# Quarter loads, an earlier first transpose and other k^T v portions in an attention and expert kernel

## The chip, the cores and the metric

The kernel runs on one core of one Trainium2 chip. The metric is the device time of one execution in microseconds (us). Engines: TensorE (PE; its weight loads are listed as PEld), VectorE (DVE), ScalarE (ACT), GpSimd (POOL), and SyncE (SP), which here does nothing but issue DMAs.

## What is computed

Linear attention with an RMS norm, then a mixture of experts with one expert for each token and a skip test. In short:

```python
kv  = einsum('bhsd,bhse->bhde', k, v)        # q, k, v: (8, 8, 576, 64) float32
o   = einsum('bhsd,bhde->bhse', q, kv)
x   = o / sqrt(mean(o*o, -1) + 1e-6) * g_norm   # then as (4608, 512)
run = x @ w_skip > 0
e   = argmax(x @ w_gate); gate = softmax(x @ w_gate)[e]
out = x + run * gate * (relu(x @ w1[e]) @ w2[e])   # 8 experts, 512 -> 1024 -> 512
```

## The kernel before

The program has two parts. The attention part takes the first 124 us of the span; the expert part takes the rest and is not touched. The order of all instructions is written out by hand (`tc.manual_schedule`): each engine works through its own queue in the order in which the program issues.

**Loads.** For each of the eight b (batches), k, v and q come as tiles `[128, 4, 9, 64]`: index j = 2u + w counts pairs of heads, and a row of one j is 9 x 64 numbers in one stretch (2,304 bytes). `load_part` (L115) moves half of such a tile, u = 0 or 1, in one DMA of 576 KB. `load_kv` (L128) issues k and v by turns, `load_q` (L136) q. All loads and most stores are on SyncE's queue. k and v have three buffers each, q has two. b = 0, 1, 2 of k and v and b = 0, 1 of q are issued at the start; the rest from the plan below.

**k^T v.** `state(b, some)` (L371) works through 18 pairs (u, c) for a b, four products for each into `sum_ps`; the first nine need u = 0 of k and v, the others u = 1. The last portion ends with ScalarE's copies into a `kvd` buffer (L386). Three short steps finish the buffer: `state_t(b)` (L389) transposes (L393) and copies (L396), `state_m(b)` (L399) multiplies by the gate weights (L402) and copies (L405), `state_s(b)` (L407) puts the result into the other half of the partitions (L411, L415).

**The 36 units.** A unit n is a fourth of a b's rows and heads; units 16, 17, 34 and 35 take the ninth column c of four b at once, from `q8s`, and need no transpose of their own. b = 0 to 7 begin at units 0, 4, 8, 12, 18, 22, 26 and 30. `turn(n)` (L451) transposes q on TensorE into the one bank of `ps_q` (L460) and copies on ScalarE (L463). `values(n)` (L486) multiplies it with `kvd` (L498, or L508 for the ninth column) into one of two banks, ScalarE squares (L514), `squares` sums on VectorE (L522), `root` is on ScalarE (L529), `norm` takes the reciprocal (L536) and the product `xl` (L545) on VectorE, which frees the bank. GpSimd adds up the logits and weighs `xl` (L597 to L615). Rows of `xb` are stored.

**The plan.** The loop over steps n (L1007) issues `turn(n + 1)`, `root(n - 1)`, the jobs "early", `values(n)`, `norm(n - 1)`, `squares(n)`, the jobs "pe", then the gating pieces for VectorE (from step 12 on for the first group, from step 22 for the second) and the jobs "end". `portions` (L963) says at which step the k^T v of a b begins and how many of its 18 pairs each step takes, at "pe". In the step after the last portion come `state_t` (early) and `state_m` (pe), a step later `state_s`. `load_kv(b + 3)` is at the "end" of the step with `state_t(b)`, `load_q(b + 2)` two steps after the b's first unit.

Ahead of the loop stand, on TensorE, filler products (`dense`), the two halves of `state(0)`, and then `turn(0)`, `state_t(0)`, `state_m(0)`, `turn(1)`, `state_s(0)` (L953 to L961).

Of the kernel before, what the change touches and what calls it, by code (L numbers as in the profile page):

```python
# [8 lines left out]
FP32 = mybir.dt.float32  # L9
# [8 lines left out]
def kernel(  # L18
# [44 lines left out]
    B, H, S, D = q.shape  # L63
    DM = H * D
    N = B * S
    P = 128
    C = S // 64
# [30 lines left out]
    kv_pool = attn.enter_context(tc.tile_pool(name="kv", bufs=3))  # L98
# [13 lines left out]

    kts, vts, qts = {}, {}, {}

    def load_part(t, src, b, u):  # L115

        js = slice(2 * u, 2 * u + 2)
        nc.sync.dma_start(
            out=t[:, js, :, :].rearrange("p j c d -> p j (c d)"),
            in_=src[b].rearrange("(j a) (p c) d -> (a p) j (c d)", a=2, c=C)[:, js, :])  # L120

    def load(pool, tag, src, b):
        t = pool.tile([P, 4, C, D], FP32, tag=tag, name=tag)
        for u in range(2):
            load_part(t, src, b, u)
        return t

    def load_kv(b):  # L128
        if b < B:
            for name, to in (("k", kts), ("v", vts)):  # L130
                to[b] = kv_pool.tile([P, 4, C, D], FP32, tag=name, name=name)
            for u in range(2):
                for src, t in ((k, kts[b]), (v, vts[b])):
                    load_part(t, src, b, u)

    def load_q(b):  # L136
        if b < B:
            qts[b] = load(q_pool, "q", q, b)
# [4 lines left out]


    load_kv(0)
    load_q(0)

# [19 lines left out]
    def dense(count, ps=warm_ps):  # L167

        for _ in range(count):
            nc.tensor.matmul(out=ps[:, :], lhsT=ones[:, :],  # L170
                             rhs=ones[:, :].unsqueeze(1).to_broadcast([P, 4, P]), start=True, stop=True)
# [33 lines left out]
    for i in range(KVD):  # L205
        t = kvd_pool.tile([P, 2, 2, 2, PK], FP32, name=f"kvd{i}")
# [87 lines left out]
    for lo, m, _ in runs:  # L294

        if m < P and (lo, m) not in again:
            t = keep.tile([P, P], FP32, name=f"again{lo}_{m}")
# [73 lines left out]
    def state(b, some):  # L371

        kt, vt = kts[b], vts[b]
        for i in some:
            u, c = divmod(i, C)
            for w in range(2):
                for a in range(2):
                    r = slice(a * 64, (a + 1) * 64)
                    nc.tensor.matmul(  # L379
                        out=sum_ps[w * 64:(w + 1) * 64, a, u, :],  # L380
                        lhsT=kt[r, 2 * u + w, c, :], rhs=vt[r, 2 * u + w, c, :],
                        start=(c == 0), stop=(c == C - 1), skip_group_check=True)
        if some.stop < 2 * C:
            return
        for w in range(2):
            nc.scalar.copy(out=own(b, w)[:, :, G:G + 2 * D].rearrange("p u (a d) -> p a u d", a=2),  # L386
                           in_=sum_ps[w * 64:(w + 1) * 64, :, :, :])

    def state_t(b):  # L389
        for u in range(2):  # L390
            for w in range(2):
                r = slice(w * 64, (w + 1) * 64)
                nc.tensor.matmul(out=kvT_ps[:, u, r], lhsT=kvds[b % KVD][:, u, w, w, G:G + 2 * D],  # L393
                                 rhs=ident[:, r], start=True, stop=True)
        kvT = att_pool.tile([P, 2, P], FP32, tag="kvT", name="kvT", bufs=1)
        nc.scalar.copy(out=kvT[:, :, :], in_=kvT_ps)  # L396
        kvTs[b] = kvT

    def state_m(b):  # L399
        kvT = kvTs.pop(b)  # L400
        for u in range(2):
            nc.tensor.matmul(out=lg_ps[:, u, :, :, :], lhsT=kvT[:, u, :], rhs=gw_b[:, u, :, :, :],  # L402
                             start=True, stop=True)
        for w in range(2):
            nc.scalar.copy(out=ends_of(own(b, w)), in_=lg_ps[w * 64:(w + 1) * 64, :, :, w, :])  # L405

    def state_s(b):  # L407

        for w in range(2):
            r, o = slice(w * 64, (w + 1) * 64), slice((1 - w) * 64, (2 - w) * 64)  # L410
            nc.tensor.matmul(out=sw_ps[o, :], lhsT=ident[r, r], rhs=own(b, w), start=True, stop=True,  # L411
                             skip_group_check=True)
        for w in range(2):
            o = slice((1 - w) * 64, (2 - w) * 64)
            nc.scalar.copy(out=kvds[b % KVD][o, :, w, 1 - w, :],  # L415
                           in_=sw_ps[o, :].rearrange("p (u k) -> p u k", u=2))
# [25 lines left out]
    def at(step, part, job):  # L442
        todo.setdefault((step, part), []).append(job)
# [7 lines left out]
    def turn(n):  # L451
        _, b, i, u = units[n]
        if i is None:
            qTs[n] = q8s[b][:, u, :, :, :]
            return
        ps = ps_q.tile([P, 2, 2, 2, 64], FP32, tag="q", name="q_ps")
        for w in range(2):
            for hf in range(2):
                c = 4 * i + 2 * hf
                nc.tensor.transpose(out=ps[:, w, :, hf, :], in_=qts[b][:, 2 * u + w, c:c + 2, :],  # L460
                                    identity=ident[:, :])
        qT = att_pool.tile([P, 2, 2, P], FP32, tag="qT", name="qT")
        nc.scalar.copy(out=qT[:, :, :, :].rearrange("p w a t -> p (w a t)"),  # L463
                       in_=ps[:, :, :, :, :].rearrange("p w a h t -> p (w a h t)"))
        qTs[n] = qT
# [353 lines left out]
    def slot_rows(cols, pool, tag):  # L819

        n = cols.stop - cols.start
        rows = pool.tile([P, n], I32, tag=f"rows{tag}", name="rows")
        nc.vector.tensor_single_scalar(out=rows[:, :], in_=srow[:, cols], scalar=float(N),
                                       op=ALU.add)
        src = pool.tile([P, n], I32, tag=f"src{tag}", name="src")
        nc.vector.scalar_tensor_tensor(out=src[:, :], in0=rows[:, :], scalar=N, in1=rows[:, :],
                                       op0=ALU.is_lt, op1=ALU.mult)
        return rows, src
# [64 lines left out]
    def early():  # L893
# [41 lines left out]
        yield "mid", put  # L935

    load_kv(1)
    load_q(1)
    load_kv(2)


# [8 lines left out]
    for n, (_, b, i, _) in enumerate(units):  # L950
        if i is not None:
# [2 lines left out]
    dense(4)  # L954
    state(0, range(C, 2 * C))
    dense(5)
    turn(0)
    state_t(0)
    state_m(0)
    turn(1)  # L960
    state_s(0)  # L961

    portions = {1: (1, (10, 8)), 2: (4, (6, 6, 6)), 3: (7, (5, 6, 7)), 4: (11, (3, 4, 4, 4, 3)),  # L963
                5: (16, (3, 2, 6, 7)), 6: (20, (4, 4, 5, 5)), 7: (24, (4, 4, 5, 5))}
    over = 0
    for b, n in starts.items():
        if b:
            step, counts = portions[b]
            i = 0
            for count in counts:  # L970
                at(step, "pe", lambda b=b, some=range(i, i + count): state(b, some))
                i += count
                step += 1
            assert i == 2 * C and step < n and step - len(counts) > over - 1
            at(step, "early", lambda b=b: state_t(b))
            at(step, "pe", lambda b=b: state_m(b))
            at(step + 1, "early" if step + 1 == n else "pe", lambda b=b: state_s(b))
            over = step
        at(over, "end", lambda b=b: load_kv(b + 3))

        at(n + 2, "end", lambda b=b: load_q(b + 2))

    def gating(g):

        yield from choose(g)
        yield lambda: rank(g)
        numbers = number(g)
        yield next(numbers)
        if g == LAST - 1:
            yield from rank_experts()  # L990
            load_weights(0, wpool_a, later=True)
        yield from numbers
        if g == LAST - 1:
            yield from early()
# [57 lines left out]
    with tc.tile_pool(name="wpool_b", bufs=1, reuse_waits="tile") as wpool_b, \  # L1052
# [491 lines left out]
        rows, src = slot_rows(slice(0, NCOL), gat_pool, "")  # L1544
# [34 lines left out]
        with tc.If(n_rounds > 1):  # L1579
            with tc.For_i(1, n_rounds, 1):  # L1580
# [12 lines left out]
                rows, src = slot_rows(slice(0, NCOL), slot_pool, "")  # L1593
# [35 lines left out]
```

## Time and profile before

| | |
|---|---|
| three runs | 375.22, 376.25, 376.61 us (median 376.25) |
| the profiled execution | 376.26 us |
| its span, first to last instruction | 374.4 us |
| TensorE clock granted | 0.996 |
| busy: PE, PEld, DVE, ACT, POOL | 97%, 84%, 65%, 39%, 33% |
| k, v, q loads: number, size | 16 each, 576 KB |
| median from issue to landing: k, v, q | 9.9, 10.7, 10.2 us |

A profile page has the busy share of each engine, the span in 40 slices of 9.4 us, a chain of work followed back from the last instruction, and groups of instructions by line. In a line of the timeline the first number is the start, the second the length from the first instruction to the end of the last, then engine, line, operation and tiles, how many, and in brackets how long the engine was idle ahead of it and what ended that.

### The profile page before, as it was taken

The page shows a single profiled execution, that of the slowest core. Times are in us where ns is not written, and L with a number is a line of the kernel's source. Part 1 is how long each engine was busy: PE and PEld are TensorE (multiplying, and loading weights), DVE is VectorE, ACT ScalarE, POOL GpSimd, SP SyncE. Part 2 cuts the span into 40 slices and gives each one's busy share as a digit, 9 for nine tenths or more (in the row PEclk, how much of TensorE's full clock was granted, in tenths as well). Part 3 has the DMA queues.
Part 4 walks back from the last instruction along what each step waited for, and adds up shares of the span by engine and source line. Part 5 has one row for each costly group of instructions (what it writes and reads, how often), then busy time and mean ns, then how long its engine had stood idle before and what let it go on. Part 6 is the DMA issues. An engine that isn't in the chain of part 4 may idle for free.

```text
span 374.4 us, 9661 instructions
## 1 busy us (share of the span) xinstructions
PE 363.2 (97%) x3859; PEld 315.2 (84%) x3859; DVE 244.3 (65%) x627; ACT 146.0 (39%) x398; POOL 123.1 (33%) x191
## 2 busy tenths in 40 slices
PE   8999999999999999999999999999999999999994
PEld 4687797898979679779879987988998998998983
DVE  2354458667878845676766675876876876878831
ACT  2366676676776222214403421430440440441420
POOL 7035457655768555223012303203202302102003
PEclk9999999999999999999999999999999999999998
DMA  7999999996499449966518263672762761700001
GB/s 290 393 391 391 401 403 394 404 384 201 130 330 311 111 109 325 395 204 226 203 53 268 69 226 103 225 254 54 259 228 47 273 230 61 269 3 32 26 1 53
DMA packets 32039, 81.70 MB, mean 218 GB/s; under 512 B 2474, under 2 KB 2482, under 8 KB 31988
## 3 DMA queue, kind: packets, MB, share of 16 engines
q1 hardware_dynamic: 28176, 69.47, 52.3%
q0 software_dynamic: 3792, 11.53, 9.2%
q8 instruction: 32, 0.52, 0.6%
q14 instruction: 19, 0.16, 0.1%
q10 hardware_dynamic: 20, 0.02, 0.0%
HBM read 66.80 MB, written 14.48 MB: 217 GB/s over the span
## 4 chain that ended last, share of the span: by engine, by line
PE 83%; issue 6%; POOL 4%; DVE 3%; ACT 3%; POOLq 0%; DVEq 0%; ACTq 0%
PE bank L1253 44%; PE bank L1185 9%; PE o_ps L498 7%; PE sum_ps L379 5%; PE bank L1173 4%; PE q_ps L460 3%; PE g_ps L393 2%; PE q_ps L170 2%; PE bank L1154 2%; POOL xb L615 2%; DVE xl L545 1%; DVE rs L522 1%; PE g_ps L411 1%; ACT qT L463 1%; ACT sq L514 1%
## 5 line engine op out<-in xcount | busy, mean ns | idle before, releaser
L1263 ACT COPY p<-bank 128x128 f32<-128x128 f32 (+6 forms) x70 | 20.8, 297 | 99.5 <-PE bank L1253 88.2
L1253 PE MATMUL bank<-xt,w 128*128 128x128 f32 (+5 forms) x336 | 55.5, 288 | 0.0
L615 POOL TENSOR_TENSOR xb<-xl,g_b 128x512 f32<-128x512 f32 x36 | 43.7, 1216 | 34.3 <-DVE rs L536 30.4
L1384 POOL DMA_INDIRECT out_dram<-xg,rows x14 | 14.0, 999 | 118.6 <-DVE xg L1381 115.4
L1253 PEld LDWEIGHTS bank<-xt,w 128*128 128x128 f32 x336 | 47.0, 190 | 1.9 <-DVE bank L1257 1.4
L1257 DVE TENSOR_TENSOR bank<-bank,p 128x128 f32<-128x128 f32 (+6 forms) x70 | 23.6, 338 | 30.2 <-PE bank L1253 29.0
L498 PE MATMUL o_ps<-kvd,qT 128*128 128x146 f32 x240 | 35.8, 290 | 1.0 <-ACT kvd L415 0.7
L1253 PE MATMUL bank<-xs,s 128*128 128x128 f32 (+5 forms) x224 | 36.7, 289 | 0.0
L522 DVE TENSOR_REDUCE rs<-sq 128x8 f32<-128x512 f32 x36 | 24.6, 682 | 15.6 <-ACT sq L514 15.5
L498 PEld LDWEIGHTS o_ps<-kvd,qT 128*128 128x128 f32 x240 | 31.6, 188 | 2.0 <-ACT kvd L415 1.5
L1253 PEld LDWEIGHTS bank<-xs,s 128*128 128x128 f32 x224 | 31.1, 190 | 1.0 <-ACT p L1263 0.8
L1185 PE MATMUL bank<-w,ht 128*32 128x128 f32 (+2 forms) x424 | 29.9, 313 | 0.0
L545 DVE TENSOR_TENSOR xl<-o_ps,rs 128x584 f32<-128x584 f32 x32 | 24.5, 767 | 4.3 <-DVE rs L536 0.5
L1185 PEld LDWEIGHTS bank<-w,ht 128*32 128x32 f32 (+2 forms) x424 | 18.2, 119 | 10.7 <-issue 7.6
L1253 PE MATMUL bank<-t,ht 128*128 128x256 f32 x112 | 27.0, 384 | 0.0
L1145 POOL DMA_INDIRECT xg<-out_dram,src x14 | 15.6, 1116 | 33.3 <-DMA out_dram<-xg,rows 18.0
L1253 PE MATMUL bank<-w,ht 128*128 128x256 f32 x112 | 26.5, 380 | 0.0
L514 ACT ACTIVATE sq<-o_ps 128x512 f32<-128x512 f32 x34 | 20.3, 597 | 15.0 <-PE o_ps L498 14.4
L379 PE MATMUL sum_ps<-v,k 64*64 64x64 f32 x1152 | 25.3, 227 | 0.4 <-issue 0.4
L1253 PE MATMUL bank<-t,hs 128*128 128x256 f32 x112 | 25.3, 379 | 0.0
L379 PEld LDWEIGHTS sum_ps<-v,k 64*64 64x64 f32 x1152 | 21.4, 138 | 4.5 <-issue 2.2
L1253 PEld LDWEIGHTS bank<-t,ht 128*128 128x128 f32 x112 | 20.8, 190 | 3.9 <-issue 1.2
(223 smaller groups left out, 679.2 us busy)
## 6 DMA issues: line engine op xcount, KB each, us to landing
w<-in_moe_w_dram SPq DMA_DIRECT2D x16, 2048.0 KB, 8.9
k<-in_k_dram SPq DMA_DIRECT2D x16, 576.0 KB, 9.9
v<-in_v_dram SPq DMA_DIRECT2D x16, 576.0 KB, 10.7
q<-in_q_dram SPq DMA_DIRECT2D x16, 576.0 KB, 10.2
out_dram<-xb SPq DMA_DIRECT2D x29, 256.0 KB, 9.8
out_dram<-xb POOLq DMA_DIRECT2D x7, 256.0 KB, 6.6
xg<-out_dram,src POOLq DMA_INDIRECT x16, 3.6
out_dram<-xg,rows POOLq DMA_INDIRECT x16, 6.2
```

The costliest lines, as they stand in the source:

```text
L379: nc.tensor.matmul(out=sum_ps[w * 64:(w + 1) * 64, a, u, :], lhsT=kt[r, 2 * u + w, c, :], rhs=vt[r, 2 * u + w, c, :], start=(c == 0), stop ...
L498: mm = nc.tensor.matmul(out=ps[:, w, 0:2 * PK].rearrange("p (r k) -> p r k", r=2)[:, :, cols], lhsT=qT[:, w, a, :], rhs=kvds[b % KVD][:, u ...
L514: nc.scalar.activation(out=sq[:, :, :, :], in_=heads(ps, G, G + 2 * D), func=ACT.Square)
L522: nc.vector.tensor_reduce(out=rs[:, :, :], in_=sq[:, :, :, :].rearrange("p x y (a d) -> p x (y a) d", a=2), axis=AX.X, op=ALU.add)
L545: nc.vector.tensor_tensor(out=xl[:, :, :, :].rearrange("p x y (a k) -> p x (y a) k", a=2), in0=ps[:, :, 0:2 * PK].rearrange("p x (h k) -> ...
L615: late.append((lambda: nc.gpsimd.tensor_tensor(out=xb[:, :, 4 * u * D:(4 * u + 4) * D].rearrange("p r (w x) -> p r w x", w=2), in0=xl[:, : ...
L1145: nc.gpsimd.indirect_dma_start(out=x_of(xg, off, m), out_offset=None, in_=cut_rows(m)[:, :], in_offset=bass.IndirectOffsetOnAxis(ap=idx[:, ...
L1173: nc.tensor.matmul(out=hps[:, cols], lhsT=w_sb[r][0][:, dc, f * P:(f + 1) * P], rhs=xt[:, dc, cols], start=(dc == 0), stop=(dc == DC - 1))
L1185: nc.tensor.matmul(out=yps[q * m:(q + 1) * m, 0:n], lhsT=ht(f)[:, off:off + m], rhs=w_sb[r][1][:, f, q * n:(q + 1) * n], start=(f == 0), s ...
L1253: nc.tensor.matmul(out=out, lhsT=lhsT(i), rhs=rhs(i), start=start and i == 0, stop=i == k - 1, skip_group_check=True)
L1257: nc.vector.tensor_tensor(out=to, in0=x, in1=y, op=ALU.add)
L1263: nc.scalar.copy(out=t, in_=x)
```

## The change

```diff
-    def load_part(t, src, b, u):
+    def load_part(t, src, b, j):
-        js = slice(2 * u, 2 * u + 2)
+        js = slice(j, j + 1)
...
     def load(pool, tag, src, b):
-        for u in range(2):
-            load_part(t, src, b, u)
+        for j in range(4):
+            load_part(t, src, b, j)
...
-    def load_kv(b):
+    def load_kv(b, js=range(4)):
         if b < B:
-            for name, to in (("k", kts), ("v", vts)):
-                to[b] = kv_pool.tile([P, 4, C, D], FP32, tag=name, name=name)
-            for u in range(2):
+            if js.start == 0:
+                for name, to in (("k", kts), ("v", vts)):
+                    to[b] = kv_pool.tile([P, 4, C, D], FP32, tag=name, name=name)
+            for j in js:
                 for src, t in ((k, kts[b]), (v, vts[b])):
-                    load_part(t, src, b, u)
+                    load_part(t, src, b, j)
...
     dense(5)
+    state_t(0)
     turn(0)
-    state_t(0)
     state_m(0)
...
-    portions = {1: (1, (10, 8)), 2: (4, (6, 6, 6)), 3: (7, (5, 6, 7)), 4: (11, (3, 4, 4, 4, 3)),
-                5: (16, (3, 2, 6, 7)), 6: (20, (4, 4, 5, 5)), 7: (24, (4, 4, 5, 5))}
+    portions = {1: (1, (10, 8)), 2: (4, (6, 6, 6)), 3: (7, (5, 6, 7)), 4: (11, (5, 6, 7)),
+                5: (16, (5, 5, 4, 4)), 6: (20, (4, 4, 5, 5)), 7: (24, (4, 4, 5, 5))}
...
-        at(over, "end", lambda b=b: load_kv(b + 3))
+        at(over, "end", lambda b=b: load_kv(b + 3, range(4 if b else 2)))
         at(n + 2, "end", lambda b=b: load_q(b + 2))
+        if b == 0:
+            at(n + 2, "end", lambda: load_kv(3, range(2, 4)))
```

Each k, v or q tile now comes in four DMAs of one j (288 KB) instead of two. `state_t(0)` is issued ahead of `turn(0)`. The fourth k and v (b = 3) are issued in two halves, j = 0 and 1 at the end of step 0 as before, j = 2 and 3 at the end of step 2, behind the third q (b = 2). The k^T v of the fifth b (b = 4) takes steps 11 to 13 instead of 11 to 15, so that its `state_t`, `state_m`, `state_s` and the load of the eighth k and v come two steps sooner. That of the sixth (b = 5) keeps its steps 16 to 19 with other counts.

## The prediction

> **What bounds the kernel now.** I read the page's slices and its DMA queue first, then the waits, then the timeline around each part of the change. Times are microseconds from the span's start.
>
> ```profile
> PE   8999999999999999999999999999999999999994
> ...
> DMA  7999999996499449966518263672762761700001
> ...
> PE 83%; issue 6%; POOL 4%; DVE 3%; ACT 3%; POOLq 0%; DVEq 0%; ACTq 0%
> ```
>
> One digit is 9.4 us. TensorE is busy nearly throughout; the DMA engines are full for the first nine slices (to about 83). Both could be the limit there, so the list of waits decides: in it no matmul waits for a load. The timeline says how close it is. SyncE's loads run at a pace of about 1.5 us for 576 KB, and from the sixth on nearly each waits for an earlier one to land (the second half of q1 is issued at 9.91, when the second half of v0 has landed: 2.27 + 7.5 = 9.8). So issue times give landing times, with some eight transfers under way:
>
> | load | landed | first used | spare |
> |---|---|---|---|
> | k0, v0 first half | 6.5 | 8.1 | 1.6 |
> | k0, v0 second half | 9.8 | 10.9 | 1.1 |
> | k1, v1 second half | 19.8 | about 21.8 (ten of 18 pairs on from 20.6) | 2.0 |
> | q2 first half | 36.5 | 37.6 (`turn(8)`) | 1.1 |
> | k3, v3 second half | 35.0 | 45 | 10 |
>
> DMA is full, but ahead. What ends late is a loop of TensorE, ScalarE and VectorE, and the change touches it in two places.
>
> At the start:
>
> ```profile
> 13.37 0.42 PEld L460 LDWEIGHTS q_ps<-ident,q 128*128 128x128 f32 x4 [0.55 <-PE q_ps L170]
> ...
> 13.87 1.00 PE L393 MATMUL g_ps<-ident,kvd 128*128 128x64 f32 x8
> ...
> 14.91 0.37 ACT L396 COPY kvT<-g_ps 128x256 f32<-128x256 f32 x1 [0.25 <-PE g_ps L393]
> ...
> 15.33 0.64 PE L402 MATMUL g_ps<-gw_b,kvT 128*128 128x36 f32 x4 [0.46 <-ACT kvT L396]
> ...
> 17.31 0.82 ACT L415 COPY kvd<-g_ps 64x292 f32<-64x292 f32 x2 [0.25 <-PE g_ps L411]
> ...
> 17.76 1.27 PE L498 MATMUL o_ps<-kvd,qT 128*128 128x146 f32 x8 [0.21 <-ACT kvd L415]
> ```
>
> `turn(0)` (L460) stands ahead of `state_t(0)` (L393), whose result goes through three ScalarE copies (L396, L405, L415) before the first values (L498). TensorE idles inside this chain.
>
> At steps 14 to 16, between 59 and 66:
>
> ```profile
> 61.78 1.24 PE L498 MATMUL o_ps<-kvd,qT 128*128 128x146 f32 x8 [0.26 <-DVE xl L545]
> ...
> 62.95 0.58 PE L379 MATMUL sum_ps<-v,k 64*64 64x64 f32 x24
> ...
> 64.11 1.19 PE L393 MATMUL g_ps<-ident,kvd 128*128 128x64 f32 x8 [0.58 <-ACT kvd L386]
> ...
> 60.00:64.00 4.00, 3.27 (x72) 2.72 (x70) 3.47 (x10) 2.28 (x7) 3.56 (x7) 1.00 1.06 392
> ```
>
> The last line is of the table by stretches: TensorE is busy 3.27 of 4 us, its weight loads 2.72, VectorE 3.47. Steps 14 and 15 have few k^T v products (four and three pairs), VectorE has the first gating pieces in the same steps, and `state_t(4)` has no q transposes ahead of it to cover the copy that it needs.
>
> **What the skill says.** "DMA: Bandwidth & Descriptors", section "Anatomy of one DMA", puts a DMA at about 2.0 us plus its bytes at 436 GB/s, by its own fit of the GpSimd path. For 576 KB that is 3.4 us; the first load here takes 4.2 and later ones 10 to 13, so nearly all of that is queueing, and half the size in flight shortens the wait without moving the data. Its section "Bandwidth" has the rule to batch to 1 MiB; this trace doesn't bear that out for loads in flight together: 389 to 408 GB/s in 576 KB pieces. "Trainium Kernel Development and Optimization", section "Key Constraints", says that all queues share the same 16 DMA engines; in the trace the queues of SyncE and GpSimd fill them together, so a reordering moves a wait and makes no bandwidth.
>
> **The change part by part.**
>
> *Four transfers for each load.* 48 loads become 96, of 288 KB, in the same order; an estimate of 0.74 us of data each. Issuing takes 0.37 to 0.47 us where nothing holds SyncE back (0.74, 1.26, 1.75, 2.27 are 0.5 apart); 0.5 is less than 0.74, so the engines stay full. Eight in flight are now 8 x 0.74 = 5.9 us instead of about 12; the smallest round trip is an estimate of 4.2 - 0.74 = 3.5 us, so 2.4 us of slack stay for a SyncE that waits. k0 and v0 have landed whole when they did before. A pair of heads starts when both halves of a former half are in, so TensorE gains nothing. The extra waits on TensorE: 16 of the former ones stand as instructions of 51 ns in front of L379; twice the transfers need 16 more, at most 16 x 0.051 = 0.8 us. The portion at 34.31, which has such a wait in its middle, lasts 0.93, just as the one at 31.65, which has it at its head, so I take nothing and keep 0.8 as the upper end. Below nothing: no gain, since no matmul waited for a load.
>
> *`state_t(0)` before `turn(0)`.* The filler matmuls end at 13.3 and the copies L386 at 12.97, so L393 runs 13.35 to 14.35 and L396 14.36 to 14.73. `turn(0)` takes 0.66 in that shadow and ends at 14.9; its copy on ScalarE lies 14.93 to 15.52. L402 can start at 14.8 instead of 15.33; its copies L405 queue behind q's, 15.52 to 15.92 (16.05 to 16.45 before). `turn(1)` has the one q bank and waits for 15.52, until 16.15. L411 starts at 16.1 (16.50), L415 at 16.9 (17.31), the values at 17.35 (17.76): **-0.4**. The ends: -0.5 if `turn(1)` isn't in the way, 0 if the later loop absorbs it.
>
> *Third q between the halves of the fourth k and v.* q2 moves ahead of two 576 KB transfers: 2 x 1.5 = 3 us earlier; the second half of k3 and v3 as much later, with 10 us to spare. q2's spare of 1.1, from which the 0.4 above is taken, grows to 3.7. On SyncE the four q issues wait for `turn(3)` (22.6), but by the eight in flight their turn comes only at about 26. **0**; were q2 left in place, 0.7 us would still cover it.
>
> *Other portions.* A pair costs 0.86 / 6 = 0.143 us (48 records, 31.72 to 32.57). b = 4 goes from 3, 4, 4, 4, 3 in steps 11 to 15 to 5, 6, 7 in 11 to 13; its `state_t` (1.18) and `state_m` (0.37) move from step 16 to 14, `state_s` (0.44) from 17 to 15; b = 5 goes from 3, 2, 6, 7 to 5, 5, 4, 4. On TensorE:
>
> - steps 11 to 13: 2, 2 and 3 pairs more, +1.0. They have no waits to hide in; step 14 starts at 60.05 for 59.04.
> - step 14: the turn covers the copies L386 (60.1 to 60.85), then `state_t`, values, `state_m` without a wait: to 63.2.
> - step 15: values to 64.3, `state_s` to 65.0. The 0.26 and 0.58 above, and the late LDWEIGHTS beside them, are gone.
> - step 16: what is late next is VectorE's `xl` of step 15. The values need a bank that it frees: square 0.60, sum 0.69, root 0.30, reciprocal 0.20, product 0.77 from 62.85 with 0.3 of queueing give 65.7, a new wait of 0.7. Then values 0.7, five pairs 0.7, ranking 0.8: step 17 starts at 68.0 for 67.77.
> - steps 17 to 19: `state_s` gone (-0.44), 3 pairs more in the first, 2 and 3 fewer after. VectorE (number and one-hot pieces, 2.7 us for each step) holds step 18, whose values wait for `xl` until 70.7. Step 20 starts at 75.0 for 75.40.
>
> Sum **-0.4**. Ends: -1.4, all idle time of steps 14 to 16 (0.16, 0.26 to 0.36, 0.58 to 0.69 and the smaller ones); +0.4, if VectorE holds steps 18 and 19 whole.
>
> The eighth k and v (b = 7) are also issued two steps sooner, ahead of three stores; those wait up to 5.9 us longer, and six `xb` buffers (12 steps) cover it. From 83 on DMA has room. After the attention part every start hangs on the step before, so -0.8 goes through.
>
> **Sum.** 376.26 (the profiled execution: 374.4 of span and 1.86 around it; the median of the runs is 376.25) - 0.4 - 0.4 = 375.4 after rounding.
>
> **Rivals.**
> A: all the idle time goes. -0.5 at the start, -1.4 in steps 14 to 16, and -0.4 for the TensorE gap at 24.2 inside a row of L379 that nothing in the profile explains: 374.0. For it: TensorE is the busiest engine and VectorE has idle time. Against: VectorE's chain from values to `xl` is 3 us long, whatever TensorE has to do.
> B: nothing gets through; ScalarE and VectorE turn the earlier start into waits of their own: 376.3. For it: ScalarE's `rs` and VectorE's reciprocal already wait in most steps.
> C: SyncE can't issue fast enough. Place: the loads after the first 16 pieces. Between 11 and 26 a 576 KB issue took 0.37 to 1.55, mean 1.1 us. If that is the price of an instruction and not of a full queue, 96 loads and 20 stores come at it: the 100 left at 9.8 us would need 100 x 1.0 = 100 us at 1.0 each, q7 would land at about 114 instead of before 102.7, and the end would be about 387. It decides from a mean of about 0.9: q3 is then the 57th, issued at 9.8 + 41 x 0.9 = 46.7, landed 4 us later, when it is needed (51.2). Against: the first loads need 0.5.
>
> **Chances.** Forecast 0.49 (own range 374.7 to 376.1), A 0.22, B 0.20, C 0.09. The range 373.6 to 376.9 takes in A, B and the 0.8 of the waits and leaves out C and the tails. Half a per cent, which a measurement can just tell from no change, is 1.9 us: below 374.4 lies A, over 378.1 lies C.
>
> **What would show it.** First values at 17.35; L379 still with no wait for a load; k, v and q landing in 5 to 7 us from issue; `state_t(4)` directly behind a turn, no wait of 0.58 at L393 near 60, a new wait of the L508 values for `xl` of about 0.7; step 20's turn 0.8 earlier (74.6). The prediction is wrong if DMA falls under 380 GB/s before 60, if SyncE's issues average 0.9, or if the later part of the span changes its length.

## The result, and the profile after

| | before | after |
|---|---|---|
| median | 376.12 us (374.97 to 377.15, 22 runs) | 375.31 us (373.76 to 376.03, 22 runs) |
| the profiled execution | 376.26 us, span 374.4 | 374.46 us, span 372.7 |

The medians differ by 0.8 us, where 0.8 was forecast and 375.4 was the number. The recorded ratio of the two sets of runs is 0.9976, 95% interval 0.9966 to 0.9986, or 0.9 us. It is not the ratio of the medians (0.9978 here), and neither are the ratios below: the runs of before bunch in two groups about 1 us apart (of the 67 beside experiments 5 to 8, 36 lie up to 375.71 and 31 from 376.11 on), and a median moves with the share of each group. The two profiles show more, 1.7 us of span, because that execution of before is 0.14 us slower than its median and that of the changed kernel 0.85 faster. Most of this section is about why that difference is not all the change's.

Line numbers in the changed kernel are one higher than in the prediction (L379 is now L380, L393 L394, L498 L499, L545 L546). The slices and the engine shares of the chain, from the page of the changed kernel:

```profile
PE   8899999999999999999999999999999999999994
...
DMA  7999999999489439955608263662662761700001
...
PE 80%; issue 6%; POOL 4%; DVE 3%; ACT 3%; DMA 2%; SPq 0%; POOLq 0%; DVEq 0%; ACTq 0%
```

DMA stays busy for one slice more (the tenth, 305 GB/s for 201 before), and the chain has a new entry, "DMA 2%": something at the start now hangs on a load. It was forecast that nothing would. The loads themselves (count, KB each, median us from issue to landing), from the page's DMA issues:

```profile
k<-in_k_dram SPq DMA_DIRECT2D x32, 288.0 KB, 6.0
v<-in_v_dram SPq DMA_DIRECT2D x32, 288.0 KB, 6.2
q<-in_q_dram SPq DMA_DIRECT2D x32, 288.0 KB, 5.9
```

Half the size lands in 6 us for 10, as the queueing argument had it, and SyncE keeps up. The first issues on SyncE's own timeline of the changed kernel:

```profile
1.67 0.48 SPq L118 DMA_DIRECT2D k<-in_k_dram  x1
2.19 0.43 SPq L118 DMA_DIRECT2D v<-in_v_dram  x1
2.66 0.43 SPq L118 DMA_DIRECT2D k<-in_k_dram  x1
3.75 0.33 SPq L118 DMA_DIRECT2D v<-in_v_dram  x1
4.65 0.33 SPq L118 DMA_DIRECT2D k<-in_k_dram  x1
```

0.33 to 0.48 us for each where nothing holds it back. But the pieces at 3.75 and 4.65 wait for an earlier transfer: they come 1.09 and 0.9 us behind the piece ahead, just when the first two pieces have landed (3.73 and 4.63 in the trace).

The start on TensorE's timeline, the counterpart of the prediction's second view:

```profile
10.55 1.26 PE L380 MATMUL sum_ps<-v,k 64*64 64x64 f32 x68 [0.85 <-DMA v<-in_v_dram]
11.75 1.25 PE L171 MATMUL q_ps<-ones 128*128 128x512 bf16 x5
12.84 1.00 PE L394 MATMUL g_ps<-ident,kvd 128*128 128x64 f32 x8
13.68 0.61 PE L461 MATMUL q_ps<-ident,q 128*128 128x128 f32 x4
14.30 0.64 PE L403 MATMUL g_ps<-gw_b,kvT 128*128 128x36 f32 x4
...
16.81 1.27 PE L499 MATMUL o_ps<-kvd,qT 128*128 128x146 f32 x8 [0.21 <-ACT kvd L416]
```

First the new wait: the second half of `state(0)` sits 0.85 us for v. Then the reordered part. `state_t(0)` (L394) follows the five fillers directly, without the 0.55 us for the q bank that stood ahead of `turn(0)` before, and `state_m(0)` (L403) no longer waits for its copy. From the start of the fillers to the first values it is 16.81 - 11.75 = 5.06 us; before it was 17.76 - 12.06 = 5.70.

Steps 14 to 16, from the timeline:

```profile
59.46 1.18 PE L394 MATMUL g_ps<-ident,kvd 128*128 128x64 f32 x8
...
64.61 0.74 PE L509 MATMUL o_ps<-kvd,q 64*64 64x73 f32 x32 [0.82 <-DVE xl L546]
```

and the same place in the table by stretches (columns: length, then busy time of PE, PEld, DVE, ACT, POOL, then clock, DMA share, GB/s):

```profile
60.00:64.00 4.00, 3.79 (x30) 3.12 (x29) 2.15 (x6) 2.57 (x8) 2.35 (x6) 1.00 1.04 389
64.00:68.00 4.00, 3.39 (x145) 3.15 (x149) 3.33 (x9) 2.46 (x7) 3.03 (x6) 1.00 1.04 410
```

`state_t(4)` has no wait any more, and TensorE is busy 3.79 of 4 us from 60 to 64 where it was 3.27. The idle time is back in the next stretch (3.39, before the change 3.84): the values of step 16 wait 0.82 us for VectorE's `xl`.

**Where the 1.7 us went.** The same events in both profiles, by subtraction:

| event | before | after | shift | added since the row above |
|---|---|---|---|---|
| first k^T v product | 8.07 | 6.91 | -1.16 | -1.16 |
| last five fillers | 12.06 | 11.75 | -0.31 | +0.85 |
| first values | 17.76 | 16.81 | -0.95 | -0.64 |
| `turn(12)` (behind the gap near 24) | 51.62 | 50.50 | -1.12 | -0.17 |
| first matmul of the expert part | 124.27 | 122.66 | -1.61 | -0.49 |
| end of the span | 374.4 | 372.7 | -1.7 | -0.1 |

The first row is no work of the TensorE edits: nothing is issued differently on TensorE ahead of it. The +0.85 behind it is the wait for v shown above. The experiments have to say what the first row is and why v comes late.

### The profile page after: what moved, and what is told of

It reads as the page before. It is cut to its first block, busy times and chain, and to the rows that moved or that the text cites. A ratio compares the mean times of both kernels' runs of the same rounds, so it can differ in the third digit from the quotient of the medians.

```text
span 372.7 us, 9717 instructions
## 1 busy us (share of the span) xinstructions
PE 361.1 (97%) x3859; PEld 314.3 (84%) x3859; DVE 243.5 (65%) x627; ACT 146.2 (39%) x398; POOL 122.7 (33%) x191
## 4 chain that ended last, share of the span: by engine, by line
PE 80%; issue 6%; POOL 4%; DVE 3%; ACT 3%; DMA 2%; SPq 0%; POOLq 0%; DVEq 0%; ACTq 0%
PE bank L1256 45%; PE bank L1188 9%; PE o_ps L499 7%; PE sum_ps L380 5%; PE bank L1176 4%; PE q_ps L461 3%; DMA v<-in_v_dram 2%; PE g_ps L394 2%; PE bank L1157 2%; POOL xb L616 2%; DVE xl L546 1%; ACT qT L464 1%; PE o_ps L480 1%; DVE rs L523 1%; ACT sq L515 1%
## 5 line engine op out<-in xcount | busy, mean ns | idle before, releaser
L499 PE MATMUL o_ps<-kvd,qT 128*128 128x146 f32 x240 | 35.8, 290 | 0.7 <-ACT kvd L416 0.7
L499 PEld LDWEIGHTS o_ps<-kvd,qT 128*128 128x128 f32 x240 | 31.6, 189 | 1.5 <-ACT kvd L416 1.5
L546 DVE TENSOR_TENSOR xl<-o_ps,rs 128x584 f32<-128x584 f32 x32 | 24.5, 767 | 4.3 <-DVE rs L537 0.5
L380 PE MATMUL sum_ps<-v,k 64*64 64x64 f32 x1152 | 24.6, 222 | 1.1 <-DMA v<-in_v_dram 0.8
L380 PEld LDWEIGHTS sum_ps<-v,k 64*64 64x64 f32 x1152 | 20.9, 134 | 4.7 <-issue 1.0
```

What stands on the lines that cost most here:

```text
L380: nc.tensor.matmul(out=sum_ps[w * 64:(w + 1) * 64, a, u, :], lhsT=kt[r, 2 * u + w, c, :], rhs=vt[r, 2 * u + w, c, :], start=(c == 0), stop ...
L499: mm = nc.tensor.matmul(out=ps[:, w, 0:2 * PK].rearrange("p (r k) -> p r k", r=2)[:, :, cols], lhsT=qT[:, w, a, :], rhs=kvds[b % KVD][:, u ...
L546: nc.vector.tensor_tensor(out=xl[:, :, :, :].rearrange("p x y (a k) -> p x (y a) k", a=2), in0=ps[:, :, 0:2 * PK].rearrange("p x (h k) -> ...
```

## The experiments

Times are compared with runs of the kernel before on the same chip. Differences of half a microsecond are near what the intervals can tell apart (each is about +-0.4 to 0.5 us), so each run is read from its profile as well.

**1. Quarter loads alone.** The kernel before with four transfers for each tile and nothing else:

```diff
-        js = slice(2 * u, 2 * u + 2)
+        js = slice(j, j + 1)
```

> The kernel before with quarter loads alone; everything else as before. Theory (the loads were ahead of TensorE, and at the start small transfers leave the DMA engines short): no gain. First half of state(0) where it was for the same clock phase, second half of v0 landing 0.5 to 0.8 us later than 9.8; time between 0 and +0.7 us against before, ratio 1.000 to 1.002. Rival (shorter queues bring the gain): ratio 0.997 to 0.999.

Measured: 376.98 against 377.17 us, ratio 0.9992 (0.9979 to 1.0005). First values at 17.70 for 17.76, 5.71 behind the fillers, and no matmul waits for a load. Alone this part is worth -0.3 us, give or take 0.5, which is not told from the forecast of nothing. In this execution the first product starts late (8.01) and v is there in time. The short supply of the theory is there: 341, 333 and 347 GB/s in the three stretches of 2 us from 4 to 10 (before: 404, 399 and 392).

**2. The order alone.**

```diff
+    state_t(0)
     turn(0)
-    state_t(0)
```

> The kernel before with state_t(0) ahead of turn(0) alone. Theory: from the start of the last five filler products to the first values 5.05 us instead of 5.70, kept to the end: -0.6 us, ratio 0.998 to 0.9985. As the prediction priced it: -0.4. Rival (ScalarE and VectorE absorb it): ratio 1.000.

Measured: 376.63 us, ratio 0.9987 (0.9976 to 0.9999). The first values come 17.22 - 12.16 = 5.06 behind the fillers. The eight profiles with this order and whole fillers have 5.05 or 5.06, the five with the old order 5.70 or 5.71: the part is worth 0.64 us whatever the loads do. And it lasts: the first values are 0.54 us earlier than in the profile before, the expert part starts 0.56 earlier.

**3. The portions alone.** The two entries of `portions` that differ:

```diff
-4: (11, (3, 4, 4, 4, 3)), 5: (16, (3, 2, 6, 7))
+4: (11, (5, 6, 7)),       5: (16, (5, 5, 4, 4))
```

> The kernel before with the other portions for b = 4 and 5 alone. Theory: the distance from step 11's turn to step 21's shorter by 0.5 us, a new wait of 0.7 to 0.8 us of the ninth column's first values for xl, ratio 0.998 to 0.9995. Rival (the new wait gives all back): ratio 1.000.

Measured: 377.69 us, ratio 1.0015 (1.0001 to 1.0029): if anything slower. From `turn(12)` to the expert part its shift against the profile before grows by 0.03 us. The wait of the step-16 values for `xl` is there, and with it a new gap of 0.36 at 73.10 (below).

**4. Order and portions, loads as before.** Edits 2 and 3 together.

> Both moves on TensorE, with the loads in halves and in the order of before. Theory: the sum of the two, -1.1 us, ratio 0.997, as fast as the full change or up to 0.3 us faster than it, since the quarter loads bring nothing. Rival (the loads are part of the gain, or the moves need them): slower than the full change by 0.3 us or more.

Measured: 376.55 us, ratio 0.9986 (0.9974 to 0.9998), the same as the order alone. From `turn(12)` to the expert part the shift goes from -0.32 to +0.43, a loss of 0.75 us. A gap of 0.80 in the middle of a portion, with no buffer or load named, is more than all of it:

```profile
71.58 0.46 PE L379 MATMUL sum_ps<-v,k 64*64 64x64 f32 x16
72.84 0.29 PE L379 MATMUL sum_ps<-v,k 64*64 64x64 f32 x4 [0.80 <-issue]
```

**5. The changed kernel again.**

> The changed kernel once more, for a second profile and a comparison on the same chip as the next three. If the early start of state(0) in the first profile (6.9 instead of 8.0 us) was the phase in which TensorE's clock rises and not the change, it stands at 8.0 here in about half the profiles, with no wait for v0, and the fillers behind it start at 12.0 to 12.3; the first values are then 5.05 us behind those. Ratio 0.9976 as before.

Measured: 375.04 against 375.53 us, ratio 0.9977 (0.9966 to 0.9988), the first result once more. Its profile starts early too (6.98), v is waited for 0.53 us, that of b = 1 another 0.49 at 21.0, and the portions give -0.48.

**6. The changed kernel with the old portions.** Edit 3 undone.

> The changed kernel with the old portions. Theory (portions are worth about 0.5 us where the loads come in quarters): 0.3 to 0.5 us slower than the changed kernel, the turns of steps 11 to 21 keep their distances of before. Rival (portions are worth nothing; e3 was 0.1% slower): as fast as the changed kernel or faster.

Measured: 375.13 us, ratio 0.9979 (0.9969 to 0.9989). In time the portions are worth 0.1 us here, with an uncertainty of about half a microsecond; in the profile the shift moves by +0.08 from `turn(12)` to the expert part, where that of the changed kernel moves by -0.49.

**7. The changed kernel with the old order.** Edit 2 undone.

> The changed kernel with turn(0) ahead of state_t(0) again. Theory: from the last fillers to the first values 5.70 us, not 5.05; 0.5 to 0.65 us slower than the changed kernel. Rival (the loop absorbs it): as fast.

Measured: 375.32 us, ratio 0.9990 (0.9976 to 1.0005). Fillers to values is 5.70 again. The ratio is 0.0013 above that of experiment 5, or 0.5 us, as the theory has it, with intervals that overlap. This profile has two of the gaps marked issue, 0.86 at 25.35 and 0.30 at 73.04.

**8. The changed kernel with k0 and v0 in halves.** The lines of `load_kv`; `load_part` takes n as the number of j:

```diff
+            n = 1 if b else 2
-            for j in js:
+            for j in js[::n]:
```

> The changed kernel with k0 and v0 in halves, all other loads in quarters. Theory (at the start the small transfers take four of the eight places, so quarters leave the DMA engines short): over 390 GB/s between 4 and 6 us instead of 292, v0 whole at 9.8 and not 10.5; where TensorE's clock rises early no wait for v0 and up to 0.7 us gained, where it rises late nothing; 0 to 0.4 us faster than the changed kernel in the median. Rival (quarters at the start cost nothing): the same time.

Measured: 375.08 us, ratio 0.9982 (0.9971 to 0.9993), no better than the changed kernel. Its timeline:

```profile
7.44 1.28 PE L381 MATMUL sum_ps<-v,k 64*64 64x64 f32 x72
10.17 1.28 PE L381 MATMUL sum_ps<-v,k 64*64 64x64 f32 x72 [0.48 <-DMA v<-in_v_dram]
```

The wait for v stays at 0.48, although k0 and v0 are issued as before the change and DMA moves 399 GB/s from 4 to 6 us. The trace has v0 whole at 10.04, for 9.79 in the first profile of before and at most 9.45 in the second (experiment 10), so a part of this wait is only the early start. So neither the size of these four transfers nor a rate that is low at 4 to 6 us is needed for the wait. The changed kernel's 292 GB/s there had suggested the rate:

```profile
4.00:6.00 2.00, 2.00 (x14) 1.32 (x12) 0.00 (x0) 0.00 (x0) 1.79 (x4) 1.00 0.95 292
```

What is common to the profiles that wait is what is queued behind v0, quarters of q and of k1. That these take bandwidth from v0 before it has landed is my guess, and no run here isolates it.

**9. The third q behind the fourth k and v again.**

```diff
-        at(over, "end", lambda b=b: load_kv(b + 3, range(4 if b else 2)))
+        at(over, "end", lambda b=b: load_kv(b + 3))
-        if b == 0:
-            at(n + 2, "end", lambda: load_kv(3, range(2, 4)))
```

> The changed kernel, but the third q stands behind all of the fourth k and v again, as before the change. My prediction put this part at nothing: the third q is needed at turn(8), about 37 from the start, and its two former halves landed at 36.5 at the latest. Theory 1 (cover is enough): no wait of turn(8) for a load, time as the changed kernel, ratio to before 0.9976. Theory 2 (cover was used up by the earlier start, since the turns now run 1.0 to 1.6 sooner): turn(8) waits 0.2 to 0.7 for q, and the time rises by as much, ratio 0.998 to 0.9995.

Measured: 376.67 against 377.60 us, ratio 0.9981 (0.9970 to 0.9993), not told apart from the changed kernel. `turn(8)` starts at 37.06 without a wait, but its third weight load waits for q:

```profile
37.53 0.20 PEld L461 LDWEIGHTS q_ps<-ident,q 128*128 128x128 f32 x2 [0.27 <-DMA q<-in_q_dram]
```

The wait of the second theory is there, at its lower end. Its price is not: from `turn(8)` to `turn(9)` it is 3.93 us, in the changed kernel 4.00. So the cover was used up, and the loop absorbed it.

**10. The kernel before, a second profile.**

> The kernel before, for a second profile, to see what differs between executions of one and the same program. If the clock's rise is tied to the program, the first k^T v product starts at 8.0 to 8.1 as in the first profile; if it depends on the execution, it can start anywhere from 6.9 to 8.1. The gap inside the second portion of b = 1 near 24 should lie behind 30 records again, its size anywhere from 0 to 0.9.

The fillers ahead of the first product, in the first profile and in this one:

```profile
6.89 1.03 PE L170 MATMUL q_ps<-ones 128*128 128x512 bf16 x2
```

```profile
6.37 0.60 PE L170 MATMUL q_ps<-ones 128*128 128x512 bf16 x2
```

The timeline of this one behind that, with the last row from much later:

```profile
7.28 1.28 PE L379 MATMUL sum_ps<-v,k 64*64 64x64 f32 x72
8.48 1.04 PE L170 MATMUL q_ps<-ones 128*128 128x512 bf16 x4
...
10.66 1.25 PE L170 MATMUL q_ps<-ones 128*128 128x512 bf16 x5
...
36.62 0.63 PE L460 MATMUL q_ps<-ident,q 128*128 128x128 f32 x4 [0.33 <-DMA q<-in_q_dram]
```

One and the same program starts its first product at 8.07 in one execution and 7.28 in another, and its last fillers at 12.06 and 10.66, 1.40 us apart. The filler matmuls show why: they take 634 ns each at first and 379 to 390 later; in this execution the step comes by 4.5, in the first profile two fillers at 6.89 still take 1.03 us (0.60 here). The Trainium skill says so of the clock, "TensorE: Matmul & The Clock Gate", section "Part 1: The HAM clock gate (the "warmup" mystery)": it rises about 4 us into the activity, give or take 500 ns, because its window runs freely. These traces agree that it varies and show more than 500 ns: under 3.5 us behind the first filler (1.07) in one execution, over 6 in another (from 5 on small products stand between the fillers here, so this isn't quite the page's steady stream). The first product comes between 7.28 and 8.07 with loads in halves, between 6.91 and 8.01 with quarters. So most or all of the table's -1.16 is the execution's. And this view shows two covers at their edge. The second half of `state(0)` starts at 9.45 (between the two filler groups shown) without a wait, so with loads in halves v0 is whole by 9.45. And an early start uses up the cover of q2: `turn(8)` waits 0.33 and starts at 36.62, which is the landing time of 36.5 in the prediction's table to 0.1. This wait too is absorbed: from `turn(7)` to `turn(9)` it is 6.40 us here and 6.38 in the first profile.

**11. What the gaps marked issue are.** The two TensorE moves, loads as before, and the last five fillers cut into twenty of a fourth of the columns: the same columns, 30 TensorE instructions more.

```diff
-    dense(5)
+    dense(5, cut=4)
```

> Both TensorE moves, loads in halves, and the last five fillers cut into twenty of a fourth of the columns (the same columns in all, 30 TensorE instructions more, nothing else changed). It asks what the TensorE gaps marked issue are. Theory 1 (late delivery of the next block of 256 TensorE instructions while the loads fill the DMA engines): the gap at about 24 moves by 30 instructions, which is 7 to 8 products or 15 records, to behind 14 to 16 records of the second portion of b = 1 (with loads in halves it lay behind 30 of them), and a gap near 73 lies at the head of the third portion of b = 5 instead of in its middle. Theory 2 (something of the data at this place, a buffer or a load): the gap stays behind 30 records.

The prediction left "the TensorE gap at 24.2" unexplained. It is there in both profiles of before and in experiments 2, 3 and 4 (0.41, 0.41, 0.61, 0.47, 0.49), always behind 30 records of the same portion, and it was absent in experiment 1. In the first profile:

```profile
23.54 0.69 PE L379 MATMUL sum_ps<-v,k 64*64 64x64 f32 x30
24.63 0.74 PE L379 MATMUL sum_ps<-v,k 64*64 64x64 f32 x34 [0.41 <-issue]
```

A record is what the profile has of one matmul instruction; a float32 product leaves two. If I count TensorE's instructions in program order, two for each record (its weight load and itself; so four for a float32 product, two for a transpose or a filler) and one for each wait that is an instruction of its own, then every such gap within k^T v lies at number 193 + 256 n, give or take one:

| n | kernel | counted product of the portion | records ahead of the gap, as measured |
|---|---|---|---|
| 2 | before (both profiles), 2, 3, 4 | 15 of 32 done | 30 of 64 |
| 2 | changed, 7, 9 (four waits more ahead of it) | 14 of 32 done | 28 of 64 |
| 2 | 8 (two waits more) | 14 of 32 done | 29 of 64 |
| 5 | 5, 12 | 23 of 24 done | 47 of 48 |
| 9 | 3, 4 | 7 of 16 done | 16 of 32 |
| 9 | 7 | 5 of 16 done | 11 of 32 |

With 30 more ahead, the gap of n = 9 has to move 7.5 products or 15 records towards the head, from behind 16 records to behind one. The timeline of experiment 11:

```profile
34.45 0.85 PE L379 MATMUL sum_ps<-v,k 64*64 64x64 f32 x41
35.62 0.34 PE L379 MATMUL sum_ps<-v,k 64*64 64x64 f32 x7 [0.32 <-issue]
...
70.80 0.69 PE L379 MATMUL sum_ps<-v,k 64*64 64x64 f32 x31 [0.59 <-issue]
```

31 of 32 records lie behind it: it moved by exactly 15. The n = 4 gap, at 35.62, is at the counted place too (20 of 24 products done, behind 41 of 48 records). At n = 2 this execution has none, so that half of the expectation was not tested.

The second theory, something in the data, falls. The page of every kernel here has a queue for instructions; first its line on the page of the changed kernel, then the same queue in experiment 4 from 70.3 to 70.5 alone:

```profile
q8 instruction: 32, 0.52, 0.5%
q8 instruction: 1, 0.02, 34.0%
```

32 packets, 0.52 MB: 16 KB for each. The Trainium skill, "Runtime: NRT & Kernel Launch", section "Instruction fetch mechanics", says that instructions are fetched in blocks of 16 KiB (256 instructions), by a DMA queue of the sequencer's own, and that crossing a boundary is "mostly hidden".

The positions agree, and the packets' times in the traces say more. The one above runs from 70.38 to 71.47, and the product behind the gap starts at 72.84. All 17 gaps at these places (one of them, 0.30 at 46.76 in experiment 3, is in a transpose of q) end 1.26 to 1.50 us behind the end of a packet of this queue. At n = 1 to 10, up to about 81 us, TensorE comes to 140 such places in the 14 profiles. At the 17 with a gap the latest packet had ended 0.14 to 0.93 us earlier, at the other 123 at least 1.06. So TensorE waits there for its block of instructions. The price isn't hidden here: 0.26 to 0.86 us where a gap shows, with DMA at 387 to 404 GB/s in the 4 us ahead of it.

Over the executions these gaps sum to 0 to 1.29 us; with loads in halves to 0.41, 0.41, 0.61, 0.91, 1.13 and 1.29, in quarters to 0, 0, 0.26, 0.26, 0.50, 0.53, 0.86 and 1.16. The means are 0.79 and 0.45; that quarters shorten the gaps is suggested and not shown. (A gap of 0.31 ahead of later fillers near 110, in seven profiles, lies at no such place, 7 us or more behind a packet, and isn't counted.)

**12. Filling the new wait.** The changed kernel, with b = 5 begun a step earlier:

```diff
-5: (16, (5, 5, 4, 4))
+5: (15, (3, 4, 4, 4, 3))
```

> The changed kernel, but b = 5 takes 3, 4, 4, 4 and 3 pairs in steps 15 to 19 instead of 5, 5, 4 and 4 in steps 16 to 19. Theory 1 (the wait of the step-16 values for xl of 0.74 to 0.82 is TensorE idle time that k^T v can fill; VectorE has room in steps 17 to 19): three pairs at 0.143 go into step 15, the wait falls from 0.8 to about 0.4, steps 17 to 19 are 0.4 shorter, the turn of step 20 comes 0.4 earlier against the first turn, the time is about 0.4 below the changed kernel (ratio to before about 0.9965). Theory 2 (VectorE's chain from values to xl sets steps 16 to 18, whatever TensorE does): what is put into step 15 is taken from the wait, and the same 0.4 shows up as longer waits for xl at steps 17 to 19: no change (0.9976).

Measured: 376.15 against 377.60 us, ratio 0.9966 (0.9956 to 0.9977), the lowest of all; next to the 0.9981 of experiment 9 on the same chip the intervals still touch. The waits that are left, from the timeline:

```profile
64.48 0.74 PE L509 MATMUL o_ps<-kvd,q 64*64 64x73 f32 x32 [0.47 <-DVE xl L546]
...
68.95 0.41 PE L480 MATMUL o_ps<-ident,q 128*64 128x128 f32 x2 [0.26 <-DVE xl L546]
```

0.82 became 0.47 and 0.26, and a small wait for ScalarE's `kvd` behind them grew to 0.17. From `turn(12)` to the expert part this kernel gains 0.66 us, 0.17 more than the changed kernel's 0.49: between the two theories. Of the 0.4 that the first theory expects, more than half is lost again to later waits.

## Why the prediction was right, and which of its steps were not

The stated 375.4 was right to 0.1 us (the sum is 375.46 before rounding, measured are 375.31), and in part that is luck. The chosen terms, -0.4 for the order, -0.4 for the portions, 0 for the loads and 0 for q2, are not those that the runs show; all four need a correction, and the errors partly cancel. By time alone, from ratios with and without a part:

| part | differences in us (experiments) |
|---|---|
| order | -0.5 (2), -0.5 (5 against 7), -1.1 (4 against 3) |
| portions | +0.6 (3), 0.0 (4 against 2), -0.1 (5 against 6) |
| loads | -0.3 (1), -0.3 (6 against 2), -0.3 (5 against 4); the last two with the move of q2, and across two chips |

Each is uncertain by half a microsecond or a little more. The order is what the time shows. The three values of the loads agree and none is clear of zero, so it stays open whether the rest of the gain is the loads' or the portions'.

**The order, -0.4: right mechanism, too small.** It measures -0.64 or -0.65 in every profile with whole fillers. The step "L393 runs 13.35 to 14.35" took the fillers' end as the start. But the 0.55 for the q bank in the prediction's own first line of that view belongs to `turn(0)`, which reuses the fillers' bank; `state_t(0)` writes another bank and needs only the copies of `kvd`, so it starts ahead of the fillers' modelled end. Counted from the start of the last fillers I had 13.35 - 12.06 = 1.29 to L393 and 17.35 - 12.06 = 5.29 to the values; measured are 1.09 and 5.06. The first difference, 0.20, is nearly all of the second, 0.23.

**The portions, -0.4: about the right size in the profiles, but not seen in the time, and the path is open.** Four profiles with the changed loads and these portions give -0.49, -0.48, -0.48 and -0.32 from `turn(12)` to the expert part, against +0.08 without the new portions. The waits came where they were put: none at `state_t(4)`, and 0.82 (forecast 0.7) for `xl` in step 16. Step 17 shifts by -0.11 (forecast +0.2), step 20 by -0.64 (forecast -0.4), and 0.16 of this is lost again by step 21. But the waits only changed places. From `turn(12)` to `turn(22)` the gaps between TensorE's products sum to 0.90 us in the profile before and 1.08 in the changed kernel's; the 0.48 us come from the 535 matmul records themselves, which follow each other closer (26.69 us without the gaps, then 26.04). No term of the prediction is that, and why they do is open.

Experiments 3, 4, 7 and 11 give +0.03, +0.75, +0.08 and +0.36 instead. Each of these four has a block gap in k^T v between 70 and 74 (0.36, 0.80, 0.30, 0.59), which none of the five profiles with the old portions has; without it they would be at -0.33, -0.05, -0.22 and -0.23. So the new portions gain some 0.2 to 0.5 us and in some executions meet a gap that eats it. The traces say how it comes there. With the new portions TensorE passes the block ahead of this place (from n = 8 to n = 9) in 5.1 to 5.2 us, with the old ones in 5.3 to 5.6. The packet of instructions starts 2.7 to 3.7 us behind n = 8, and in the four with a gap it started at 3.2 or later. So the new portions leave the block less time; what delays its packet in some executions is open.

**Quarter loads, 0: not told from nothing, wrong in a step.** "k0 and v0 have landed whole when they did before" failed. With halves v0 is whole at 9.79 in the first profile and by 9.45 in experiment 10. With quarters the wait ends between 10.02 and 10.55 in four profiles (waits of 0.17, 0.31, 0.53, 0.85) and at 10.17 in experiment 8: 0.2 to 1.1 later. It costs nothing where the clock rises late and `state(0)` gets there at 10.8 to 11.2, as in experiments 1, 6 and 7, and it takes back 0.2 to 0.9 of what an early rise gives. The prediction's own table had a spare of 1.1 there, measured in one execution with a late rise; it took that for a property of the kernel. b = 1 can wait too, 0.49 in experiment 5 and 0.19 in 9. The extra waits on TensorE (nine more instructions in the trace, where 16 were reckoned with) cost nothing visible, as chosen; four of them move the block boundary near 24 by a product.

**q2, 0: right in time; the reason given holds for a late start alone.** The prediction left 0.7 of spare; where the start comes sooner there is none, and the old place of q2 then waits 0.33 (experiment 10) or 0.27 (9). Neither wait shows at `turn(9)`, so there the loop makes this 0, and the move is at most an insurance.

**The rivals.** A wanted all idle time of steps 14 to 16, and the gap at 24.2. The first fell to the wait that was forecast, 0.82; the gap is not idle time that scheduling removes, but a block boundary. B wanted nothing to get through: the order's gain reaches the expert part whole (experiment 2), which then takes 250.1 us in the profile before and 250.0 after. C priced an issue at 1.0 when it is 0.33 to 0.48; the mean of 1.1 between 11 and 26 was the full queue's.

**The signs.** "L379 with no wait for a load" was the one that came out wrong, and "DMA falls under 380 GB/s before 60" did happen, at 4 to 6 us (292) and 8 to 10 (361), where it matters least for the total and most for v0.

## What to carry to other kernels

Compare events from a mark behind the start-up (fillers to first values, step 12 to step 20) before crediting an edit with a difference of two spans: one program's start moved by 1.4 us between two executions. A spare read from one profile is a spare of that execution; ask what it is if the start comes a microsecond sooner. When a step is moved, ask for it anew which bank and which copy it needs: the wait that stood at this place may belong to its neighbour.

## What the runs showed of the hardware

Gaps marked issue inside runs of equal matmuls can be placed by counting: they lie multiples of 256 TensorE instructions apart, last 0.26 to 0.86 us with DMA at 387 to 404 GB/s, end 1.26 to 1.50 us behind the end of a 16 KB packet of the instruction queue, and one moved by 30 instructions when 30 were added ahead of it.

The expert part, which no edit touches, took 250.0 to 250.3 us from its first matmul to the end of the span in six profiles and 251.1 to 252.0 in the other eight, with the change and without. Experiments 5 to 8, on one chip, lie on the one side, 1 to 4 and 9 to 12, on two others, on the other side. What differs is open; each time is therefore set against the kernel before on the same chip, and profiles are compared by events of the attention part.
